# Window attention and two gated MLPs on one core: new planner constants, a new order, and rotated operand slots

## The chip, the cores and the metric

The program runs on one core of a Trainium2 chip. The metric is device time in microseconds (us) of one execution; lower is better. Engines are named as in the profile: PE (matrix products), DVE (vector), ACT (activations, with function tables that have to be loaded), POOL (a slower second vector engine), SP (issues the DMAs). Each engine works through its own queue in order and waits on semaphores for the others.

## What is computed

The reference is windowed causal attention (4 batches, 8 heads, 576 positions, head size 64, window 128, a linear bias by head), then two MLPs over the 2304 x 512 result, with 2048 hidden features each:

```python
scores = np.where(mask, scale * q @ k.T + bias, -1e9)      # mask: 0 <= i - j < 128
attn = exp(scores - max) / (sum + 1e-9);  x = attn @ v     # heads side by side: 2304 x 512
h = x @ w_in;  x = (h * np.tanh(softplus(h))) @ w_out       # first MLP
h = x @ w_in2; x = np.where(h > 0, h, np.exp(h) - 1) @ w_out2  # second MLP
```

## The kernel before

**Products.** All MLP products are done in a two-level scheme with 7 products of half-size blocks in place of 8 (steps P1 to P7, in the order P1, P5, P6, P2, P7, P3, P4). Each factor is split into a high and a low part in a rounded float32 type, and three partial products (high-high, high-low, low-high) are summed. So every operand of PE needs a first half, the rounded copy (ACT, or DVE), and a second half, the difference (DVE, or POOL where both are in SBUF). `split` (L540) emits the two; `copy` (L528) and `combine` (L533) give the engines that may do them.

**Stages.** Attention of batch 0 comes first (`unit`, L687: scores, two transposes, values). Then the hidden products of the first MLP run over 4 chunks of tokens, one per batch (blocks H00 to H03, `hidden`, PE line L914, six matmuls of 288 columns a block), with the attention of the next batch between them. Next come the outward products of the first MLP in 3 chunks (O00 to O02, `outward`, PE line L1001, twelve matmuls of 384 columns a block), the hidden products of the second MLP (H10 to H12, L914 with 384 columns), and its outward products (O10 to O12). The hidden results go through DRAM (`gate`, `graw`); in the first MLP ACT applies Mish to them when they come back (L978). A block's name ends in its step: O00P5 is step P5 of outward chunk 0.

**Weights.** `convert` (L583) turns the packed 64-bit input words into float32 weights: a load, a Prelu on ACT (L593), a Copy on ACT or DVE (L597), a shift on DVE (L601), an add on POOL or DVE (L604), then four sums of blocks (DVE or POOL). Groups c0 to c3 are the four weight matrices; c0 is done at the start, the others beside the chunks. `load_weights` (W1 to W3) brings the finished ones back and splits them.

**Order.** Nothing is written out by hand in its final order. `Plan` collects about 4,100 operations with the engines that may do each (`ways`), a cost, a due time, a size for DMAs, and the function table that an ACT operation needs. `Plan.order` then runs a list scheduler over a model of the engines, whose choices set the order of each queue and the engine of each operation with more than one way. The model's constants are `LATENCY`, `LOAD`, `RATE` and the `*_cost` functions; the preferences are the table `AT`; and `SHIFT` adds a number to the priority of each group of operations. Where PE would idle in the first 90 us of the model, it gets products of constants that nobody reads (L489).

**Slots.** Buffers come from rings of slots; the next buffer of a ring takes the next slot, and its first writer waits until the last reader of the slot's former buffer is done. The split operands of the outward products (`hl`) use ring "L", with 5 slots: three on the right (numbers 4 to 6 of `right_s`), then two on the left (4 and 5 of `wide_s`). The first step of chunk 0 uses ring "L0", the same three slots on the right alone:

```python
    plan.ring("L0", right_s[4:])
    plan.ring("L", right_s[4:] + wide_s[4:])
```

Of ACT's operations, Exp is entered with the table "exp" and Mish with "mish"; the Prelu of `convert` is entered with none.

## Time and profile before

| | |
|---|---|
| time, median of 3 runs | 868.26 us (867.78 to 868.77) |
| time of the profiled execution | 868.03 us |
| its span, first to last instruction | 866.3 us |
| PE busy | 843.4 us, 97% |
| DVE busy | 723.1 us, 83% |
| ACT busy | 628.3 us, 73% |
| POOL busy | 132.4 us, 15% |
| PE share of the chain that ended last | 70% |

The time of the profiled execution is 1.73 us above its span. Busy PE counts matmuls that overlap each other, so a block of 12 matmuls of 384 columns is best timed from the start of one block to the start of the next.

### The profile page before, as it was taken

Reading aid. Unit: us, or ns where it says so; the run is one execution under the profiler, and the core shown is the slowest. Engines: PE = TensorE matmul, PEld = TensorE weight load, DVE = VectorE, ACT = ScalarE, POOL = GpSimd, SP = SyncE. Lnnn points to the kernel's source line nnn. Section 1 sums busy time; section 2 is a strip of 40 time slices with the busy share of each in tenths; the row PEclk is TensorE's granted clock in tenths of the full one; section 3 lists DMA queues with packets and bytes.
Section 4 is the critical chain, followed back from the end, with each engine's and each line's share of the span. In section 5 each row is a group of like instructions: output and inputs, shape, how many; then the busy total and the mean of one; then the engine's idle time right before and its main releaser. Section 6 shows DMA issues by size and latency. Waiting matters only on the chain.

```text
span 866.3 us, 15682 instructions
## 1 busy us (share of the span) xinstructions
PE 843.4 (97%) x5403; PEld 794.1 (92%) x5403; DVE 723.1 (83%) x1590; ACT 628.3 (73%) x1421; POOL 132.4 (15%) x115
## 2 busy tenths in 40 slices
PE   9988999999999999899899999999999999999998
PEld 6767788898889999899899999989999999999998
DVE  8999998778877689799889988895978988877863
ACT  6989997677767688875897868976998944333442
POOL 0434120000003000135213043121300000000000
PEclk9999999999999999999999999999999999999999
DMA  7436667877867886674677778676778957226102
GB/s 277 138 119 214 190 211 244 280 267 258 253 225 246 286 290 235 233 254 149 232 264 258 254 249 284 218 266 214 261 253 275 313 182 229 105 96 229 41 1 73
DMA packets 85967, 187.67 MB, mean 217 GB/s; under 512 B 8576, under 2 KB 30080, under 8 KB 85888
## 3 DMA queue, kind: packets, MB, share of 16 engines
q1 hardware_dynamic: 85888, 186.68, 64.2%
q8 instruction: 42, 0.69, 0.3%
q14 instruction: 37, 0.30, 0.1%
HBM read 117.44 MB, written 69.21 MB: 215 GB/s over the span
## 4 chain that ended last, share of the span: by engine, by line
PE 70%; DVE 12%; ACT 11%; DMA 3%; issue 3%; POOL 0%; SPq 0%; DVEq 0%; ACTq 0%; POOLq 0%
PE oA L1001 19%; PE hA L914 16%; PE oC L1001 11%; PE hC L914 8%; PE hB L914 4%; PE oB L1001 4%; PE ps_o L828 3%; DMA raw<-in_w_dram 2%; PE ps_s L725 2%; DVE hl L534 2%; PE ps_t L780 2%; DVE graw L534 1%; ACT hl L529 1%; ACT p L745 1%; ACT p L760 1%
## 5 line engine op out<-in xcount | busy, mean ns | idle before, releaser
L914 PE MATMUL hA<-xt,w 128*128 128x288 f32 (+1 forms) x1344 | 232.9, 319 | 2.3 <-ACT g L529 1.7
L529 ACT ACTIVATE hl<-graw 128x768 fp32r<-128x768 f32 x161 | 134.9, 843 | 128.1 <-PE oA L1001 63.8
L1001 PE MATMUL oA<-hl,w 128*128 128x384 f32 x1152 | 215.2, 338 | 4.2 <-DVE hl L534 2.4
L914 PEld LDWEIGHTS hA<-xt,w 128*128 128x128 f32 x1344 | 209.4, 189 | 8.0 <-ACT g L529 3.7
L534 DVE TENSOR_TENSOR hl<-graw,hl 128x768 fp32r<-128x768 f32 x168 | 165.8, 996 | 52.7 <-ACT hl L529 52.3
L1001 PEld LDWEIGHTS oA<-hl,w 128*128 128x128 f32 x1152 | 202.6, 188 | 7.0 <-DVE hl L534 4.8
L914 PE MATMUL hC<-xt,w 128*128 128x288 f32 (+1 forms) x672 | 119.7, 317 | 0.2 <-DVE g L897 0.2
L1001 PE MATMUL oC<-hl,w 128*128 128x384 f32 x576 | 111.0, 343 | 4.3 <-DVE hl L534 2.4
L1001 PEld LDWEIGHTS oC<-hl,w 128*128 128x128 f32 x576 | 103.0, 190 | 6.7 <-DVE hl L534 4.1
L914 PEld LDWEIGHTS hC<-xt,w 128*128 128x128 f32 x672 | 104.6, 188 | 3.0 <-issue 1.0
L534 DVE TENSOR_TENSOR graw<-graw 128x768 f32<-128x768 f32 x96 | 92.7, 977 | 4.2 <-ACT graw L978 1.8
L604 POOL TENSOR_TENSOR bits<-bits,raw 128x512 int32<-128x512 int32 x34 | 56.1, 1655 | 254.0 <-DVE bits L601 134.7
L529 ACT ACTIVATE g<-hA 128x288 f32<-128x288 f32 (+1 forms) x144 | 61.0, 434 | 26.6 <-PE hA L914 25.3
L745 ACT ACTIVATE p<-p,st 128x128 f32<-128x128 f32 x144 | 56.4, 396 | 13.8 <-DVE st L741 13.3
L534 DVE TENSOR_TENSOR w<-w 128x512 fp32r<-128x512 f32 x84 | 59.3, 730 | 6.2 <-ACT w L529 5.6
L914 PE MATMUL hB<-xt,w 128*128 128x288 f32 (+1 forms) x336 | 60.5, 317 | 2.4 <-DVE g L897 2.1
L914 PEld LDWEIGHTS hB<-xt,w 128*128 128x128 f32 x336 | 52.5, 188 | 4.2 <-DVE g L897 2.4
L1001 PE MATMUL oB<-hl,w 128*128 128x384 f32 x288 | 54.3, 338 | 0.0
L1001 PEld LDWEIGHTS oB<-hl,w 128*128 128x128 f32 x288 | 50.9, 188 | 0.2 <-DVE hl L534 0.2
L529 ACT ACTIVATE w<-w 128x512 fp32r<-128x512 f32 x83 | 49.3, 625 | 1.2 <-DMA w<-w_in 1.0
L896 ACT ACTIVATE e<-e 128x384 f32<-128x384 f32 x96 | 49.1, 529 | 0.7
L593 ACT ACTIVATE raw<-raw 128x512 f32<-128x512 f32 x64 | 43.0, 675 | 8.0 <-DMA raw<-in_w_dram 7.5
(100 smaller groups left out, 1109.2 us busy)
## 6 DMA issues: line engine op xcount, KB each, us to landing
graw<-gate SPq DMA_DIRECT2D x96, 384.0 KB, 4.6
raw<-in_w_dram SPq DMA_DIRECT2D x64, 512.0 KB, 5.3
gate<-g SPq DMA_DIRECT2D x64, 288.0 KB, 3.6
gate<-g SPq DMA_DIRECT2D x48, 384.0 KB, 3.9
w<-w_out SPq DMA_DIRECT2D x56, 256.0 KB, 4.0
qkv<-in_qkv_dram SPq DMA_DIRECT2D x16, 512.0 KB, 4.9
w_out<-bits SPq DMA_DIRECT2D x32, 256.0 KB, 5.1
w<-w_in SPq DMA_DIRECT2D x28, 256.0 KB, 3.7
```

What stands on the lines that cost most here:

```text
L529: ways = [("act", act_cost(n, sbuf), lambda: nc.scalar.activation(o(), i(), AF.Copy), 0.0), ("dve", dve_cost(n, sbuf), lambda: nc.vector.t ...
L534: emit = lambda eng: eng.tensor_tensor(out=o(), in0=x(), in1=y(), op=op)
L593: act(DM, lambda raw=raw: nc.scalar.activation(raw()[:, :, 1].bitcast(F32), raw()[:, :, 1].bitcast(F32), AF.Prelu, scale=2.0 ** -112, alph ...
L604: add = lambda eng, raw=raw, bits=bits: eng.tensor_tensor(out=bits().bitcast(I32), in0=bits().bitcast(I32), in1=raw()[:, :, 0].bitcast(I32 ...
L725: nc.tensor.matmul(pss[j]()[:, n, w0:2 * P], qs()[rs, n * P:(n + 1) * P], ks()[rs, ko + w0:ko + 2 * P], start=n == 0, stop=True, skip_grou ...
L745: act(P, lambda n=n, j=j: nc.scalar.activation(prob()[:, n, j], prob()[:, n, j], AF.Exp, scale=-1.0, bias=st()[:, 0, n, j:j + 1], accum_ou ...
L760: ("act", act_cost(P, True, 1), lambda y=y, f=f: nc.scalar.activation(y(), y(), AF.Copy, scale=f()), AT["norma"]),
L780: nc.tensor.transpose(ps()[:, j], prob()[:, n, j], ident)
L828: nc.tensor.matmul(o()[j * D:(j + 1) * D, c0:c0 + math.prod(y.shape[1:])], vn()[:kr, n, j], y, start=n == 0, stop=n == nkb - 1, skip_group ...
L896: act(T, lambda: nc.scalar.activation(e(), e(), AF.Relu, scale=-1.0, bias=1.0), (), [e], due)
L914: nc.tensor.matmul(ps(), w()[:, a, wi, cs], x()[:, b, k], start=step in FIRST and k == 0 and m == 0, stop=k == 1 and m == 2, skip_group_ch ...
L1001: nc.tensor.matmul(bk[name, d](), w()[:, a, wi, cs], x()[:, b, k], start=step in FIRST and f + k == 0 and m == 0, stop=f + k == NQ - 1 and ...
```

## The change

The kernel's operations are the same; the engine of some of them, their order, and the slots of `hl` differ. The change replaces all of `SHIFT`, and some of `AT` (`turn` 0.99 to 7.6, the price of a table load; `held` 10.7 to 102.2, the price of starting a DVE operation that shares a port while POOL works; `ahead`, `kappa`, `lag`, `dma`). In the model all latencies grow by 0.05 us, a DMA issue costs 0.43 us in place of 0.1, data land 0.45 us later behind their issue, and the DMA rate rises from 270 to 390 KB a us. The Prelu of `convert` is now entered with the table "exp". Ring "L" becomes one ring for each outward layer, "La" and "Lb", which begin at different slots.

```diff
-AT = dict(... turn=0.99, held=10.7, ... kappa=1.29, lag=0.9, ... dma=-14.73, ... ahead=7.48, hb=5)
+AT = dict(... turn=7.60436, held=102.159, ... kappa=1.35238, lag=0.940919, ... dma=-7.29047, ... ahead=-153.07, hb=5, lrot=2)
 SHIFT = {
-    "H000P1": -7.2, "H001P1": 4.9, "H001P6": 13.2, "H002P4": -0.5, "H002P6": -1.8, "H003P7": 0.4, "H003d": 11.8,
+    "H000P1": -15.5, "H000P2": 52.4, "H000P3": -45.1, "H000P4": -13.3, "H000P5": -21, "H000P6": -39.5, "H000P7": -1.9,
...
-    LATENCY = dict(pe=0.2, act=0.16, dve=0.13, pool=0.1, sp=0.0)
+    LATENCY = dict(pe=0.25, act=0.21, dve=0.18, pool=0.15, sp=0.05)
-    WARM = 6.9
+    WARM = 4.0
-    LOAD = 1.4
-    RATE, OUTSTANDING, LANDING = 270e3, 8, 1.9
+    LOAD = 1.3
+    RATE, OUTSTANDING, LANDING = 390e3, 8, 1.9
-                        dma_free = max(dma_free, end + 0.3) + o["moved"] / self.RATE
+                        dma_free = max(dma_free, end + 0.75) + o["moved"] / self.RATE
...
-    plan.ring("L", right_s[4:] + wide_s[4:])
+    ls, lr = wide_s[4:] + right_s[5:] + right_s[4:5], int(AT["lrot"])
+    plan.ring("La", ls)
+    plan.ring("Lb", ls[lr:] + ls[:lr])
...
-        plan.op([("sp", 0.1, emit, 0.0)], reads, writes, due=due, moved=moved * slow)
+        plan.op([("sp", 0.43, emit, 0.0)], reads, writes, due=due, moved=moved * slow)
...
                 raw()[:, :, 1].bitcast(F32), raw()[:, :, 1].bitcast(F32), AF.Prelu, scale=2.0 ** -112, alpha=-2.0 ** 32),
-                (), [(raw, 1)], due)
+                (), [(raw, 1)], due, extra=0.5, table="exp")
...
-                x = buf("L0" if at_end else "L1" if layer and ci == 0 and i == 0 else "L", (2, 2, T), F32R, "hl")
+                x = buf("L0" if at_end else "L1" if layer and ci == 0 and i == 0 else ("La", "Lb")[layer], (2, 2, T), F32R, "hl")
```

Numbers of instructions: POOL's tensor operations go from 105 to 94, ACT's activations from 1266 to 1238, DVE's operations from 1446 to 1485 (two-part ones counted once), the unread products on PE from 155 to 146, and ACT's table loads behind the first from 10 to 14. Rounded copies of `hl` on DVE (CAST hl) go from 7 to 23.

**Place 1: PE at the start of the first outward stage.** oA, oB and oC are the accumulators of the steps: the first four blocks on oA are P1, those on oC P5, the next on oA P6. Before:

```order
L914 MATMUL hC<-xt,w 128x288 x6
L1001 MATMUL oA<-hl,w 128x384 x12
L914 MATMUL hA<-xt,w 128x288 x6
L1001 MATMUL oA<-hl,w 128x384 x36
L1001 MATMUL oC<-hl,w 128x384 x24
L1001 MATMUL oA<-hl,w 128x384 x12
L1001 MATMUL oC<-hl,w 128x384 x12
```

In the changed kernel the same stretch reads:

```order
L956 MATMUL hA<-xt,w 128x288 x6
L1043 MATMUL oA<-hl,w 128x384 x24
L1043 MATMUL oC<-hl,w 128x384 x12
L1043 MATMUL oA<-hl,w 128x384 x12
L1043 MATMUL oC<-hl,w 128x384 x12
L1043 MATMUL oA<-hl,w 128x384 x12
L1043 MATMUL oC<-hl,w 128x384 x24
```

P1 was four blocks in a row (with one hidden block among them) ahead of the first P5; now P5 blocks stand between the P1 blocks, on slots that the rotated ring gives them.

**Place 2: ACT's table loads between the rounded copies of `hl`.** The queue of ACT at the second and third load of the kernel before (graw is the Mish on hidden results, raw the conversion of weights):

```order
L529 ACTIVATE hl<-graw 128x768
L593 ACT_TABLE_LOAD
L593 ACTIVATE raw<-raw 128x512
L597 ACTIVATE raw<-raw 128x512
L529 ACTIVATE hl<-graw 128x768
L593 ACTIVATE raw<-raw 128x512
L597 ACTIVATE raw<-raw 128x512
L978 ACT_TABLE_LOAD
L978 ACTIVATE graw<-graw 128x768
L529 ACTIVATE hl<-graw 128x768
```

In the changed kernel the first pair of loads that stands among the outward blocks of this chunk:

```order
L571 ACTIVATE y<-oA 128x384 x2
L635 ACT_TABLE_LOAD
L635 ACTIVATE raw<-raw 128x512
L571 ACTIVATE hl<-graw 128x768 x2
L1020 ACT_TABLE_LOAD
L1020 ACTIVATE graw<-graw 128x768
L571 ACTIVATE hl<-graw 128x768
```

and, in the second chunk, the densest group of loads in it:

```order
L571 ACTIVATE hl<-graw 128x768 x2
L1020 ACT_TABLE_LOAD
L1020 ACTIVATE graw<-graw 128x768 x2
L639 ACTIVATE raw<-raw 128x512
L635 ACT_TABLE_LOAD
L635 ACTIVATE raw<-raw 128x512
L1020 ACT_TABLE_LOAD
L1020 ACTIVATE graw<-graw 128x768 x2
L571 ACTIVATE hl<-graw 128x768 x2
```

A load is now kept apart from its neighbours by copies of `hl` in the first chunk; in the second, three loads stand without a copy of `hl` between them.

**Place 3: POOL's first work behind its setup.** Before:

```order
L604 TENSOR_TENSOR bits<-bits,raw 128x512 x2
L534 TENSOR_TENSOR sums<-bits 128x256
L604 TENSOR_TENSOR bits<-bits,raw 128x512
L534 TENSOR_TENSOR bits<-bits 128x256
L534 TENSOR_TENSOR w<-bits,w 128x512 x2
L534 TENSOR_TENSOR sums<-bits,sums 128x256 x2
L534 TENSOR_TENSOR xc<-xc 128x2x288
```

In the changed kernel:

```order
L646 TENSOR_TENSOR bits<-bits,raw 128x512
L576 TENSOR_TENSOR w<-bits,w 128x512
L576 TENSOR_TENSOR w<-sums,w 128x512
L576 TENSOR_TENSOR w<-sums,w 128x256
L576 TENSOR_TENSOR w<-bits,w 128x512
L576 TENSOR_TENSOR sums<-bits 128x256
L646 TENSOR_TENSOR bits<-bits,raw 128x512
```

Adds and sums of the first conversions have gone from POOL's queue to DVE's. Counted up to what the last block of hidden chunk 0 (H007P4) needs, POOL has 24 operations in place of 30, DVE 410 instructions in place of 400, ACT 289 in place of 294, and on PE that block is the 155th in place of the 152nd (unread products left out).

## Rows read from the trace of the kernel before

**Rows 1.** Windows by stage: length, busy us (instructions) by engine, PE clock, DMA share, GB/s
```profile
0.00:130.00 130.00, 122.19 (x969) 97.01 (x970) 122.28 (x487) 114.36 (x380) 35.96 (x40) 1.00 0.57 192
130.00:310.00 180.00, 179.73 (x1406) 162.99 (x1405) 140.30 (x466) 130.96 (x386) 13.47 (x11) 1.00 0.78 258
310.00:500.00 190.00, 183.62 (x1024) 180.79 (x1023) 171.06 (x207) 151.66 (x219) 41.64 (x30) 0.99 0.71 240
500.00:681.00 181.00, 177.95 (x999) 176.33 (x999) 151.49 (x266) 151.95 (x329) 41.31 (x34) 0.99 0.76 254
681.00:866.00 185.00, 179.88 (x1012) 176.99 (x1010) 137.95 (x168) 79.33 (x112) 0.00 (x0) 1.00 0.39 134
```

**Rows 2.** PE's waits from 310 to 510 us: total us, times, longest
```profile
PE oC L1001 <- DVE hl L534: 2.1, 3, 1.3
PE oC L1001 <- ACT hl L529: 1.9, 2, 1.0
PE oA L1001 <- ACT hl L529: 1.8, 1, 1.8
PE oA L1001 <- DVE hl L534: 0.6, 1, 0.6
```

**Rows 3.** Timeline of PE, 300 to 345 us: start, us, operation, count, idle before
```profile
312.98 6.51 PE L1001 MATMUL oA<-hl,w 128*128 128x384 f32 x36
320.42 0.44 PE L1001 MATMUL oC<-hl,w 128*128 128x384 f32 x1 [0.93 <-ACT hl L529]
321.42 5.85 PE L1001 MATMUL oC<-hl,w 128*128 128x384 f32 x23 [0.56 <-DVE hl L534]
```

**Rows 4.** Windows beside and in the two clock dips (columns as in group 1)
```profile
322.00:325.50 3.50, 3.50 (x13) 3.50 (x12) 3.50 (x5) 3.31 (x5) 0.00 (x0) 0.51 1.03 394
325.50:331.00 5.50, 5.50 (x33) 5.50 (x33) 4.80 (x6) 3.66 (x6) 0.00 (x0) 1.00 1.05 406
584.90:588.30 3.40, 3.40 (x13) 3.40 (x12) 1.59 (x3) 1.61 (x5) 0.00 (x0) 0.50 0.95 298
```

**Rows 5.** Timeline of all engines, 345 to 361 us
```profile
345.47 1.28 ACT L593 ACT_TABLE_LOAD   x1
346.76 0.69 ACT L593 ACTIVATE raw<-raw 128x512 f32<-128x512 f32 x1
349.88 1.28 ACT L978 ACT_TABLE_LOAD   x1
355.75 0.44 PE L1001 MATMUL oC<-hl,w 128*128 128x384 f32 x1 [1.00 <-ACT hl L529]
357.44 2.21 PE L1001 MATMUL oC<-hl,w 128*128 128x384 f32 x11 [1.25 <-DVE hl L534]
```

**Rows 6.** Timeline of all engines, 414 to 430 us
```profile
417.83 1.28 ACT L593 ACT_TABLE_LOAD   x1
420.38 1.28 ACT L978 ACT_TABLE_LOAD   x1
424.77 0.44 PE L1001 MATMUL oA<-hl,w 128*128 128x384 f32 x1 [1.76 <-ACT hl L529]
425.76 2.18 PE L1001 MATMUL oA<-hl,w 128*128 128x384 f32 x11 [0.55 <-DVE hl L534]
```

**Rows 7.** Timeline of all engines, 574 to 586 us
```profile
580.80 1.47 POOL L604 TENSOR_TENSOR bits<-bits,raw 128x512 int32<-128x512 int32 x1
581.05 2.04 DVE L534 TENSOR_TENSOR x<-x 128x768 f32<-128x768 f32 x1
583.61 1.32 PE L914 MATMUL hB<-xt,w 128*128 128x384 f32 x6 [2.09 <-DVE g L897]
```

**Rows 8.** PE's waits from 681 us to the end
```profile
PE oA L1001 <- DVE hl L534: 1.9, 3, 1.0
PE oC L1001 <- DVE hl L534: 0.2, 1, 0.2
```

**Rows 9.** Groups by line and form: busy us, mean ns of one, idle before
```profile
L529 ACT ACTIVATE hl<-graw 128x768 fp32r<-128x768 f32 x161 | 134.9, 843 | 128.1 <-PE oA L1001 63.8 <-PE oC L1001 39.5 <-PE oB L1001 11.5
L534 DVE TENSOR_TENSOR hl<-graw,hl 128x768 fp32r<-128x768 f32 x168 | 165.8, 996 | 52.7 <-ACT hl L529 52.3
L593 ACT ACT_TABLE_LOAD x5 | 6.4, 1283 | 0.4 <-DMA raw<-in_w_dram 0.3
L534 DVE TENSOR_TENSOR sums<-bits,sums 128x256 f32<-128x256 f32 x17 | 7.6, 446 | 0.1
L534 DVE TENSOR_TENSOR w<-sums,w 128x512 fp32r<-128x512 f32 x6 | 4.1, 678 | 0.0
```

More of the change, by code (lines that the diff above doesn't have):

```diff
@@ L20 @@
 GROUPS = ((0, 256, 0, 256), (256, 256, 128, 384), (512, 64, 384, 192))
-AT = dict(copy=2.27, both0=-0.71, both1=-8.32, both2=-3.61, turn=0.99, held=10.7, fill=90, enough=1.5, norma=-0.5, normp=2.42,
-          kappa=1.29, lag=0.9, first=-64.52, unit=2.69, h1=50.67, chunk=70.1, lead=30.24, dt=1.35, dma=-14.73,
-          conv=-27.63, wadd=-0.1, soft0=0, soft1=0, soft2=0, soft3=0, eq=4, ep=2, et=6, er=3, eb=0, eraw=3, side0=1,
-          side1=2, depth=4, ahead=7.48, hb=5)
+AT = dict(copy=2.27, both0=-0.71, both1=-8.32, both2=-3.61, turn=7.60436, held=102.159, fill=90, enough=1.5, norma=-0.5,
+          normp=2.42, kappa=1.35238, lag=0.940919, first=-64.52, unit=2.69, h1=50.67, chunk=70.1, lead=30.24, dt=1.35,
+          dma=-7.29047, conv=-27.63, wadd=-0.1, soft0=0, soft1=0, soft2=0, soft3=0, eq=4, ep=2, et=6, er=3, eb=0,
+          eraw=3, side0=1, side1=2, depth=4, ahead=-153.07, hb=5, lrot=2)
 SHIFT = {
[55 rows of a table removed]
[95 rows of a table added]
 class Slot:
@@ L362, in mm_cost @@
 def mm_cost(n):
-    return 0.000417 * n + (0.0125 if n < 384 else 0.0153)
+    return 0.000417 * n + (0.013 if n < 384 else 0.0158)
 def act_cost(n, sbuf=False, extra=0):
-    return 0.000833 * n + 0.052 + 0.041 * sbuf + 0.093 * extra
+    return 0.000833 * n + 0.049 + 0.041 * sbuf + 0.093 * extra
 def dve_cost(n, fast=False, extra=0):
-    return (0.00052 if fast else 0.001042) * n + 0.068 + 0.062 * extra
+    return (0.00052 if fast else 0.001042) * n + 0.068 + 0.067 * extra
 def pool_cost(n):
@@ L591, in convert @@
             dma(P * DM * 8, lambda raw=raw, s=s: nc.sync.dma_start(out=raw().rearrange("p n w -> p (n w)"), in_=s),
[L592 removed]
+                (), [(raw, 0), (raw, 1)], due, 1.15)
             act(DM, lambda raw=raw: nc.scalar.activation(
                 raw()[:, :, 1].bitcast(F32), raw()[:, :, 1].bitcast(F32), AF.Prelu, scale=2.0 ** -112, alpha=-2.0 ** 32),
[L595 removed]
+                (), [(raw, 1)], due, extra=0.5, table="exp")
             ends_of = lambda raw=raw: (raw()[:, :, 0].bitcast(I32), raw()[:, :, 0])
[L597 removed]
+            plan.op([("act", act_cost(DM, True, 0.5), lambda ends_of=ends_of: nc.scalar.activation(*ends_of(), AF.Copy, scale=2.0 ** -29), 0.0),
                      ("dve", dve_cost(DM, True), lambda ends_of=ends_of: nc.vector.tensor_scalar(
@@ L606, in convert @@
             plan.op([("pool", pool_cost(DM), lambda add=add: add(nc.gpsimd), 0.0),
-                     ("dve", 0.16 + 0.00104 * DM, lambda add=add: add(nc.vector), AT["wadd"])],
+                     ("dve", 0.07 + 0.00104 * DM, lambda add=add: add(nc.vector), AT["wadd"])],
                     [(raw, 0)], [bits, (bits, 0), (bits, 1)], due=due, port=True)
@@ L640, in convert @@
                 out=to, in_=(t() if n == 3 else t().bitcast(F32).rearrange("p (n c) -> p n c", n=2))),
-                [have[x][1] for x in which.split()], [("wsd", w, q, x) for x in which.split()], due, 1.2)
+                [have[x][1] for x in which.split()], [("wsd", w, q, x) for x in which.split()], due)
     def weight_slots(w):
@@ L699, in unit @@
         t = buf("qkv" + late, (cut[3],), F32, "qkv")
-        dma(P * cut[3] * 4, lambda: nc.sync.dma_start(out=t(), in_=src), (), [t], t0 - 10)
+        dma(P * cut[3] * 4, lambda: nc.sync.dma_start(out=t(), in_=src), (), [t], t0 - 10, 1.08 if part == 1 else 1.0)
         qs, ks, vs = ((lambda i=i: t()[:, cut[i]:cut[i + 1]]) for i in range(3))
```

2 lines of the change are left out of this document (removed), and 148 rows, old and new, of the table SHIFT.

## The prediction

> **What bounds the kernel now.** I read the windows by stage first [rows 1]. PE is busy almost throughout: from 130 to 310 us it misses 0.27 us of 180. So a new order of the same work can only win what PE loses elsewhere: 130 - 122.19 = 7.8 us before 130 us, 190 - 183.62 = 6.4 us in the first outward stage (310 to 500), 181 - 177.95 = 3.05 us in the second hidden stage, and in the last stage the 2.1 us of waits that are listed [rows 8]; the rest of that stage's idle time is the ending, which the change does not touch. To this come two dips of the granted clock to half, at 322 to 325.5 and at 584.9 to 588.3 us [rows 4]. Full speed beside the first is 33 matmuls in 5.5 us, 0.167 us each; 3.5 us would give 21, and 13 stand there, so a dip costs 8 x 0.167 = 1.3 us. Each followed idle PE: 0.93 us ahead of 320.42 and 0.56 ahead of 321.42 [rows 3], and 2.09 ahead of 583.61 [rows 7].
>
> In the first 130 us the queues behind PE are full themselves: DVE is busy 122.28 us, ACT 114.36 [rows 1]. There DVE and ACT, not PE, set the pace.
>
> In the first outward stage PE's waits are all for the split operand hl [rows 2]: 2.1 + 1.9 + 1.8 + 0.6 = 6.4 us, the whole loss. They are three places.
> (a) At 320 us: 0.93 + 0.56 = 1.5 us and the dip of 1.3 [rows 3, 4]. Ring L0 has three slots, so the fourth P1 operand takes the first slot again; ring L begins with that slot too, so the first P5 operand cannot be made before PE has finished the block directly ahead. The path from one block to the next is then a rounded copy on ACT (0.84 us) and a difference on DVE (1.0 us) [rows 9], with nothing to hide them.
> (b) At 355 us: 1.00 + 1.25 us [rows 5]. Two table loads with two conversions of weights stand in ACT's queue just ahead; the old planner gave Prelu no table and did not know of them.
> (c) At 424 us: 1.76 + 0.55 us [rows 6], the same with the loads at 417.83 and 420.38.
> Together (b) and (c) are 4.6 us.
>
> **The change, part by part.** *Slots and order at the start of the stage (a).* The rotated ring gives the first P5 operands the two left slots, which no P1 operand used, and PE's queue now has P1, P1, P5, P1, P5. The fourth P1 operand still waits for the first P1 block, but two blocks lie between them. A block is 12 matmuls at 0.176 us (36 of them took 6.5 us with the drain at their end [rows 3]), about 2.1 us; two give 4.2 us of cover against 0.84 + 1.0 us of split plus handovers. So 1.5 us go, and the dip's 1.3 with them: -2.8 us. What is late next is DVE: differences, weight splits and sums of hidden blocks queue there, and summed along its queue it stays about 0.5 to 3 us ahead of PE through this chunk. Should that lead fail, the wait comes back at P7 of chunk 0.
>
> *Table loads (b, c).* The loads rise from 10 to 14, 4 x 1.283 = 5.1 us more work for ACT [rows 9]. ACT is busy 151.66 of 190 us here [rows 1], so the work itself fits. What counts is whether a load stands on the path to the next hl. In chunk 0 two copies of hl now stand between a load and the next. In chunk 1 the densest group has no hl for three loads, four Mish and two conversions. Mish takes about as long as the copy of hl (both 768 wide: 0.84 us, 0.75 taking the overlap of neighbours off), a conversion 0.69 [rows 5], about 0.56 the same way: 3 x 1.29 + 4 x 0.75 + 2 x 0.56 = 8 us. By the slots of the new order, the copy ahead of the group can start when a certain PE block ends, and the copy behind it only when the fourth block after that one ends: 4 x 2.1 = 8.4 us. So the group fits, narrowly. I take (b) and (c) as gone but for 1.5 us of new tight places: in chunk 2 two pairs of blocks (P7, P3) get their operand's slot only two blocks ahead, with splits of the next weights between them on DVE. With the 0.3 us of small waits kept, the stage keeps about 2.0 of its 7.7 us: -5.7 us. Bounds: all 7.7 gone, or the loads' extra 5.1 us on the path.
>
> *Second hidden stage.* The 2.09 us wait [rows 7] came from a DVE operation of 2.04 us beside a POOL operation, ahead of the gate that frees a PSUM bank. The order of that stage is another throughout, and DVE has about 4 us less in its queue there, done earlier, where DVE idled (140.30 busy of 180 us [rows 1]). Nothing ties the old wait to the new order, and nothing forbids a like one. Of 3.05 + 1.3 = 4.35 us I keep 2.0: -2.35. Bounds: -4.35 and 0.
>
> *Start of the last stage.* Of the 2.1 us [rows 8] I keep 1.0: -1.1. DVE has its first two hl operands ready earlier, but its queue runs within about 1 us of PE afterwards. Bounds: -2.1 and +1.
>
> *First 130 us.* POOL loses 6 operations up to the last block of hidden chunk 0, and DVE has 10 instructions more. Six at 0.45 to 0.68 us [rows 9], and four short ones at 0.2 to 0.3, make some 4.5 us. PE has three blocks more in front of that block (two or three of them hidden ones, about 3 us), so DVE's surplus over PE grows by about 1.5 to 2 us. Against it, POOL operations slow DVE: one took 2.04 us beside POOL [rows 7] and about 1.0 us is usual for its size [rows 9], so six fewer can give up to 6 us back. Fewer unread products (146 for 155) cost and bring nothing, since they fill idle PE. I take +1.0; bounds -4 and +3.7 (DVE's surplus and no relief).
>
> *The rest.* The cost and latency constants, the DMA issue time and rate are only in the model; they act through the order that is counted above. DMA loads keep their distance: counted in PE blocks between the one that frees a buffer and the one that needs it, the tightest weight load of the first outward stage has 6.4 us in both orders.
>
> Sum: -5.7 - 2.35 - 1.1 + 1.0 = -8.15 us. Against the profiled execution's 868.03 us (span 866.3) that is 859.9. The median of the runs is 0.2 us higher, less than these terms are known to.
>
> Where POOL's traffic slows DVE, the Trainium skill (GPSIMD Engine Reference, Key points) says that the two share their SBUF interfaces and that DVE instructions in a 2-port mode or with two SBUF inputs contend; the 2.04 us operation [rows 7] has two SBUF inputs and agrees.
>
> **The rivals.** *DVE becomes the bound (slower).* DVE gets 39 operations more. The places where it is nearly full are the first 130 us (94% busy) and the first outward stage (171.06 of 190, 90%) [rows 1], where 7 rounded copies of hl stand on it in place of 2. If POOL's relief fails, the early +3.7 comes out in full; and if the hl waits are DVE's (2.7 of the 6.4 us already are [rows 2]), then five more copies at about 0.6 us, 3 us, add to them and the waits stay. That is 868.0 + 3.7 + 3 = 874.7, or 870.9 with half of the stage's 7.7 us gone. It decides where DVE's idle time in the outward stage falls under about 10 us. For it: the shares named. Against it: the sum of DVE's queue between the stage's first blocks and its last is within 1 us of the old, as other work was moved ahead.
>
> *Loads on the path.* The order sets 14 loads for 10; with 5.1 us of them on the path to hl the result is 859.9 + 5.1 = 865.0. For it: the group of three in chunk 1. Against it: 8 us against 8.4. The Trainium skill (ScalarE: Activation LUTs, Table sets: the hidden batching unit) tells to do all work of one set together, which this order does less than the old. The same page (What ACT_TABLE_LOAD costs) puts a switch at 1283 ns and a drain of about 1380, which would make four switches 10.6 us, an estimate from that page, and the time 870.5; here the next ACTIVATE starts 1.29 us behind the load [rows 5], with no drain to be seen.
>
> *One stall for another.* PE's waits move to other blocks and sum to the same: 868, within 1.7.
>
> *More than I take.* All waits for hl and the gate go (7.7 + 4.35 + 2.1) and the early stretch gains 1: 868.03 - 15.1 = 852.9.
>
> **How the numbers follow.** Faster or slower by 0.2% (1.7 us) is about what a measurement of this kernel can tell from no change. The forecast as summed, 856 to 863: 0.50. Loads on the path: 0.10. More than I take: 0.15. One stall for another: 0.09. DVE the bound: 0.16. So faster 0.75, same 0.09, slower 0.16. The range goes from 851.5 (below the best case) to 870.0, and leaves out about half of the DVE case and little else.
>
> **What would show it.** In the profile of the changed kernel: no idle PE and no half clock at the first blocks on oC (if there is, the slot step was wrong); PE's waits for hl in the first outward stage at about 2 us, none behind a table load (if a wait for ACT's hl stands behind the group of three in chunk 1, the cover was counted wrong); PE's idle time in the second hidden stage near 2 us; DVE's idle time in the first outward stage well above 10 us; the last block of hidden chunk 0 within about 2 us of the old, three blocks of work allowed for. The prediction is wrong if DVE is late at most blocks of either full stretch, or if the first 130 us move by more than 4 us.

## The result and the profile after

The changed kernel takes 861.28 us (median of 8 runs, 859.09 to 865.26) against 868.38 us for the kernel before on the same chip (8 runs, 867.23 to 870.48): a ratio of 0.9917, interval 0.9895 to 0.9939. The profiled execution of after took 861.93 us (span 860.2), that of before 868.03 (span 866.3). So the pair of profiles that is read below differs by 6.1 us, the medians by 7.1.

Windows by stage of after, the answer to [rows 1]: length, busy us (instructions) of PE, PEld, DVE, ACT and POOL, PE clock, DMA share, GB/s. The last two rows stand where the two dips of [rows 4] stood.

```profile
0.00:130.00 130.00, 121.55 (x977) 98.38 (x978) 121.99 (x495) 114.10 (x377) 29.02 (x34) 1.00 0.56 190
130.00:310.00 180.00, 178.34 (x1397) 162.03 (x1396) 148.19 (x490) 137.38 (x394) 18.60 (x17) 1.00 0.88 293
310.00:500.00 190.00, 185.17 (x1040) 182.34 (x1039) 177.24 (x219) 152.06 (x216) 41.49 (x28) 1.00 0.70 234
500.00:681.00 181.00, 179.51 (x1018) 177.61 (x1017) 146.59 (x259) 147.32 (x322) 27.04 (x25) 1.00 0.70 240
681.00:860.00 179.00, 172.12 (x970) 169.85 (x968) 137.45 (x171) 67.05 (x93) 0.00 (x0) 1.00 0.36 126
320.00:332.00 12.00, 12.00 (x70) 12.00 (x70) 11.90 (x16) 11.99 (x22) 0.00 (x0) 1.00 1.05 405
582.00:592.00 10.00, 10.00 (x59) 10.00 (x58) 5.34 (x11) 6.94 (x16) 3.10 (x4) 1.00 0.48 172
```

Subtract PE's busy time from each length: PE is idle for 8.45, 1.66, 4.83, 1.49 and 6.88 us, where before it was 7.81, 0.27, 6.38, 3.05 and 5.12. The sum is 23.3 us against 22.6: **the idle time of PE did not fall**. What fell is its busy time, from 843.4 to 836.7 us on the two pages. Both dips are gone (the clock column is 1.00 in the last two rows). A dip is 3.5 us in which PE works at 1.2 GHz in place of 2.4, so it does 1.75 us of work too little: 3.5 us for the two. The unread products fell from 155 to 146, and their busy time from 23.2 to 21.2 us: 2.0. About 1.2 us is left; what it is was not settled (the ends of matmuls in a profile are modelled). This is the account of one pair of profiles, and single runs of the changed kernel differ from one another, as the second profile of it shows below.

The start of the first outward stage (PE's timeline: start, us, operation, count, idle before) answers [rows 3]: P1, P1, P5, P1, P5 without a gap.

```profile
309.76 4.41 PE L1043 MATMUL oA<-hl,w 128*128 128x384 f32 x24
314.01 2.27 PE L1043 MATMUL oC<-hl,w 128*128 128x384 f32 x12
316.12 2.28 PE L1043 MATMUL oA<-hl,w 128*128 128x384 f32 x12
318.24 2.27 PE L1043 MATMUL oC<-hl,w 128*128 128x384 f32 x12
```

PE's waits in that stage, 310 to 510 us (total us, times, longest), the answer to [rows 2]: the three places of before are gone, and nine waits stand there, the longest 1.1 us for 1.8. They sum to 6.0 us for 6.4; the wait for g, 1.1 us, comes behind 500 us.

```profile
PE oA L1043 <- DVE hl L576: 1.9, 4, 0.9
PE hA L956 <- ACT g L571: 1.1, 1, 1.1
PE oB L1043 <- DVE hl L576: 1.1, 1, 1.1
PE oC L1043 <- DVE hl L576: 0.7, 1, 0.7
PE oC L1043 <- ACT hl L571: 0.7, 1, 0.7
PE oA L1043 <- ACT y L571: 0.5, 1, 0.5
```

Where they come from is seen in the densest group of table loads. The timeline of all engines of after, 395 to 422 us, cut to what bears on hl:

```profile
400.89 0.85 ACT L571 ACTIVATE hl<-graw 128x768 fp32r<-128x768 f32 x1 [1.78 <-PE oA L1043]
400.96 0.43 SPq L633 DMA_DIRECT2D raw<-in_w_dram  x1
...
404.64 0.85 ACT L1020 ACTIVATE graw<-graw 128x768 f32<-128x768 f32 x1 [0.74 <-DMA graw<-gate]
...
406.19 2.07 DVE L576 TENSOR_TENSOR hl<-graw,hl 128x768 fp32r<-128x768 f32 x1
...
407.87 0.69 ACT L639 ACTIVATE raw<-raw 128x512 int32<-128x512 uint32 x1 [2.38 <-DMA raw<-in_w_dram]
...
413.35 1.56 ACT L571 ACTIVATE hl<-graw 128x768 fp32r<-128x768 f32 x2
...
414.23 0.44 PE L1043 MATMUL oC<-hl,w 128*128 128x384 f32 x1 [0.66 <-ACT hl L571]
...
415.36 4.29 PE L1043 MATMUL oC<-hl,w 128*128 128x384 f32 x23 [0.69 <-DVE hl L576]
```

From the copy at 400.89 to the one at 413.35 pass 12.5 us. They hold 9.3 us of work, the first copy's 0.85 included (the forecast counted 8, without that copy), and 3.1 us of waits (0.74 + 2.38) **for DMAs**: ACT works in order, so a conversion of a weight whose bytes have not landed holds every copy of hl behind it. The slot for the second copy was free at 409.3, four blocks on; the copy came 4 us later, and PE's lead absorbed all but the 0.66 + 0.69 us. (The split at 406.19 took twice its usual 1.0 us; a POOL operation of 1.50 us began at 405.94.) ACT's waits from 310 to 505 us show how common this is (total, times, longest). Two rows of after:

```profile
ACT raw L639 <- DMA raw<-in_w_dram: 7.9, 5, 3.2
ACT graw L1020 <- DMA graw<-gate: 3.5, 5, 1.0
```

and one of before (its Prelu has line 593):

```profile
ACT raw L593 <- DMA raw<-in_w_dram: 1.8, 1, 1.8
```

11.4 us in place of 2.1 (with 0.3 us of before ahead of a table load). What these waits cost PE does not follow from their sum, since ACT may have time to spare where it waits; the experiments below take them apart from the loads. The same kind of wait stands in the last stage on DVE: after's timeline, 704 to 728 us.

```profile
719.43 0.96 DVE L576 TENSOR_TENSOR graw<-graw 128x768 f32<-128x768 f32 x1 [1.97 <-DMA graw<-gate]
...
723.73 0.41 PE L1043 MATMUL oA<-hl,w 128*128 128x384 f32 x1 [1.52 <-DVE y L576]
...
724.97 2.20 PE L1043 MATMUL oA<-hl,w 128*128 128x384 f32 x11 [0.82 <-DVE hl L576]
```

The difference graw<-graw at 719.43 is for an operand of the next chunk; the split hl that PE wants at 724 stands behind it in DVE's queue. Before lost 2.1 us to waits of this stage [rows 8], after 3.3 (1.5 + 1.5 + 0.3 in its list of waits).

In the groups of after that answer the first two of [rows 9], one copy of hl takes 842 ns and one split 1005, within 1% of those of before, so nothing of the gain comes from faster copies and splits.

### The profile page after: what moved, and what is told of

The parts are those of the page before. It is cut to its first block, busy times and chain, and to the rows that moved or that the text cites. A ratio compares the mean times of both kernels' runs of the same rounds, so it can differ in the third digit from the quotient of the medians.

```text
span 860.2 us, 15671 instructions
## 1 busy us (share of the span) xinstructions
PE 836.7 (97%) x5394; PEld 790.2 (92%) x5394; DVE 731.5 (85%) x1629; ACT 617.9 (72%) x1397; POOL 116.2 (14%) x104
## 4 chain that ended last, share of the span: by engine, by line
PE 60%; DMA 13%; DVE 12%; ACT 7%; issue 6%; POOL 1%; SPq 1%; ACTq 0%; DVEq 0%; POOLq 0%
PE hA L956 20%; PE hC L956 10%; PE oA L1043 9%; PE oC L1043 5%; PE hB L956 5%; DMA graw<-gate 4%; DVE hl L576 3%; PE ps_o L870 3%; DMA qkv<-in_qkv_dram 3%; PE ps_s L767 2%; DVE graw L576 2%; DMA raw<-in_w_dram 2%; DVE w L576 2%; PE oB L1043 2%; PE ps_t L822 2%
## 5 line engine op out<-in xcount | busy, mean ns | idle before, releaser
L956 PEld LDWEIGHTS hA<-xt,w 128*128 128x128 f32 x1344 | 207.3, 188 | 9.7 <-ACT g L571 3.6
L571 ACT ACTIVATE hl<-graw 128x768 fp32r<-128x768 f32 x145 | 121.1, 842 | 111.1 <-PE oA L1043 58.0
L576 DVE TENSOR_TENSOR hl<-graw,hl 128x768 fp32r<-128x768 f32 x168 | 166.6, 1005 | 28.4 <-ACT hl L571 27.7
L1043 PE MATMUL oC<-hl,w 128*128 128x384 f32 x576 | 108.8, 339 | 1.7 <-DVE hl L576 1.0
L646 POOL TENSOR_TENSOR bits<-bits,raw 128x512 int32<-128x512 int32 x30 | 47.7, 1591 | 296.0 <-DVE bits L643 176.0
L787 ACT ACTIVATE p<-p,st 128x128 f32<-128x128 f32 x144 | 56.2, 395 | 10.6 <-DVE st L783 10.4
L576 DVE TENSOR_TENSOR w<-w 128x512 fp32r<-128x512 f32 x84 | 56.7, 698 | 1.6 <-ACT w L571 1.5
L802 ACT ACTIVATE p<-p,st 128x128 f32<-128x128 f32 x124 | 41.1, 396 | 8.9 <-DVE st L797 8.8
```

The costliest lines, as they stand in the source:

```text
L571: ways = [("act", act_cost(n, sbuf), lambda: nc.scalar.activation(o(), i(), AF.Copy), 0.0), ("dve", dve_cost(n, sbuf), lambda: nc.vector.t ...
L576: emit = lambda eng: eng.tensor_tensor(out=o(), in0=x(), in1=y(), op=op)
L646: add = lambda eng, raw=raw, bits=bits: eng.tensor_tensor(out=bits().bitcast(I32), in0=bits().bitcast(I32), in1=raw()[:, :, 0].bitcast(I32 ...
L787: act(P, lambda n=n, j=j: nc.scalar.activation(prob()[:, n, j], prob()[:, n, j], AF.Exp, scale=-1.0, bias=st()[:, 0, n, j:j + 1], accum_ou ...
L802: ("act", act_cost(P, True, 1), lambda y=y, f=f: nc.scalar.activation(y(), y(), AF.Copy, scale=f()), AT["norma"]),
L956: nc.tensor.matmul(ps(), w()[:, a, wi, cs], x()[:, b, k], start=step in FIRST and k == 0 and m == 0, stop=k == 1 and m == 2, skip_group_ch ...
```

## The experiments

For most of them the order of one kernel was written out as a list and played back instruction for instruction, so that nothing but the named edit differs. Labels that begin with b start from the kernel before, those with a from the changed one. A ratio is against the kernel before, measured beside it on the same chip. In small order diffs the names are those of the timeline.

**The changed kernel again, no edit.**

> The changed kernel once more, for a second trace of it and as the measure for its three variants. 861.3 us; if the wait on landing graw at 717 to 725 us is the order's, it stands again with 2 to 3 us of PE's time; if it is an accident of one run, it is under 1 us here.

862.03 us (7 runs, 860.79 to 871.18), ratio 0.9934 (0.9913 to 0.9954). The run that was profiled was the slowest, 871.18. Its three dips (windows, columns as above) and the idle time of PE ahead of them (PE's timeline):

```profile
176.00:179.50 3.50, 3.50 (x21) 2.80 (x18) 2.07 (x13) 0.60 (x3) 0.00 (x0) 0.52 0.96 321
514.00:517.50 3.50, 3.50 (x13) 3.50 (x12) 1.13 (x4) 1.01 (x2) 0.90 (x2) 0.53 0.91 302
732.50:736.00 3.50, 3.50 (x12) 3.50 (x13) 1.35 (x2) 0.00 (x0) 0.00 (x0) 0.53 1.02 336
```
```profile
174.41 1.05 PE L956 MATMUL hC<-xt,w 128*128 128x288 f32 x6 [1.46 <-DVE g L576]
512.95 4.98 PE L956 MATMUL hA<-xt,w 128*128 128x384 f32 x18 [2.53 <-ACT g L571]
731.24 0.42 PE L1043 MATMUL oA<-hl,w 128*128 128x384 f32 x1 [1.06 <-DVE y L576]
```

Most waits of the program stand again where they stood (the third row is the one of 723.73 above). The one of 512.95 was 1.13 us in the first profile, and the one of 174.41 was not there. The dips are all new: the same program had none in its first profile and three in this one. So dips belong to a run, and each of these came right after PE had been idle. The stretch that was full in before shows a difference too:

```profile
130.00:310.00 180.00, 175.81 (x1360) 158.66 (x1361) 145.64 (x485) 134.97 (x390) 18.45 (x17) 0.99 0.85 284
```

PE is idle there for 4.19 us in place of 1.66. In all eight profiles with the new order it is idle in this stretch for 1.66 to 4.99 us, in all six that start from before for 0.16 to 0.29. PE's waits name the landing of qkv in each of the eight (1.0 to 2.9 us, none in the six), and the wait for DVE's g that stands at 174.41 here is in five of them (1.1 to 1.7 us).

**(a), the slot alone.** The first P5 operands of the first outward layer get slots that no P1 operand used; the order stays.

```diff
-    plan.ring("L", right_s[4:] + wide_s[4:])
+    plan.ring("La", [the slots written out: w5 r5 r6 w4 r4, repeated; then as before])
```

> The kernel before with its order kept, instruction for instruction; only the slots of the split operand change: up to the 24th operand of the first outward stage the first left slot and the last right slot are exchanged, so that the first P5 operand takes a slot that no P1 operand used. Theory A, the slot alone makes place (a): the 1.5 us of idle PE at 320 to 322 us and the dip of the clock behind it go, -2.8 us, 866.0. Theory B, the queues of ACT and DVE, written in an order that counted on the old slot, hold the copy back: the idle time stays above 1 us and the total within 1 us of 869.

866.62 us (12 runs), ratio 0.9981 (0.9962 to 1.0). PE at the place of [rows 3], and the window there:

```profile
319.17 0.44 PE L1001 MATMUL oC<-hl,w 128*128 128x384 f32 x1 [0.46 <-ACT hl L529]
```
```profile
319.00:325.50 6.50, 5.78 (x31) 5.53 (x32) 5.81 (x8) 5.67 (x10) 0.00 (x0) 1.00 1.01 375
```

The slot alone takes a third of the 1.5 us of idle time (0.46 + 0.55 are left), and in this profile the first dip; the copy is still made right behind the block ahead. The changed kernel, which has the order P1, P1, P5 as well, has neither. The second dip stands (its granted clock is 0.57 from 582.5 to 586.5 us), and PE's idle time in the whole stage, 6.57 us, is that of before. About 2 us in the median, on the edge of what can be told from nothing.

**The dips alone.** Unread products are put into the two idle places of before (8 at 319 us, 18 at 581); the waits for data stay.

```diff
+  8 products of ones, unread, ahead of the first P5 block     (PE, line 489)
+ 18 products of ones, unread, ahead of the block at 583.61    (PE, line 489)
```

> The kernel before with 8 unread products more in PE's queue ahead of the first P5 block and 18 more ahead of the block that waits at 583.6 us; all else as it was. Theory A, the clock falls because PE is idle there: both dips go, -1.3 us each, 866.5, while the blocks' waits stay. Theory B, the dips have another cause: they stay, and the total is 869 or more by what the products delay.

867.92 us (12 runs), ratio 0.9992 (0.9974 to 1.0011). In the profile both places run at full clock:

```profile
322.00:325.50 3.50, 3.50 (x22) 3.50 (x21) 3.50 (x5) 3.01 (x5) 0.00 (x0) 1.00 1.02 390
582.00:592.00 10.00, 10.00 (x62) 9.88 (x61) 4.72 (x10) 6.12 (x14) 0.00 (x0) 1.00 0.71 245
```

So in this run PE, kept busy, keeps its clock there: 22 matmuls in 3.5 us against 13 [rows 4]. The total did not follow: in seven of the other eleven runs the mean clock was 0.995 to 0.998, so dips came in them too, at places that no trace shows. That the filling is what kept the clock is not shown by one profile, since the same idle places pass without a dip in other runs (next experiment). What a single dip's removal brings to the median stays open.

**The loads out of before.** Prelu becomes Copy, a function of the set that Mish uses: 8 of the 10 loads go, the order stays.

```diff
-  AF.Prelu, scale=2.0 ** -112, alpha=-2.0 ** 32)
+  AF.Copy, scale=2.0 ** -112)
```

> The kernel before in its order, with Copy in place of Prelu for the converted weights' upper halves, so that 8 of its 10 table loads behind the first fall away (left out: the sign of negative weights). Theory A, as I forecast: the stalls at 355 and 424 us were the loads', 2.3 us each; both shrink under 0.5 us, -4 to -4.6, 864.5. Theory B, they are DVE's or the order's: at most 1 to 2 us go, 867 to 868.

860.16 us (6 runs), ratio 0.9919 (0.9892 to 0.9947): as much as the whole change brings. First outward window, and the longest wait left, which is not followed by a dip:

```profile
310.00:500.00 190.00, 187.98 (x1063) 186.20 (x1062) 176.46 (x217) 144.69 (x217) 47.62 (x34) 1.00 0.73 248
```
```profile
576.04 1.33 PE L914 MATMUL hB<-xt,w 128*128 128x384 f32 x6 [2.07 <-DVE g L897]
```
```profile
577.00:580.50 3.50, 3.50 (x22) 3.41 (x21) 1.92 (x4) 2.33 (x5) 0.00 (x0) 1.00 0.99 302
```

Idle PE in the stage falls from 6.38 to 2.02 us, of which 1.5 us are place (a), as in before:

```profile
319.49 0.44 PE L1001 MATMUL oC<-hl,w 128*128 128x384 f32 x1 [0.93 <-ACT hl L529]
```

That (b) and (c) come from the loads is shown: of the 4.6 us counted 0.5 is left. The median falls by 8.6 us. Part of that is dips: between runs at full clock on this chip it is 5.7 us (865.5, four runs, and 859.9, four runs). The profile of this run has no dip: PE goes on at full clock after 2.07 us of idle time, where 2.09 us in before was followed by one [rows 7, 4], and also after the 0.93 + 0.56 us of place (a), which a dip followed in before and in the run without POOL's traffic, and none here or in the run with only the count.

**The loads out of after.** The same edit in the changed kernel: 2 loads for 14.

> The changed kernel's order, instruction for instruction, but the converted weights' upper halves go through Copy in place of Prelu, so that ACT keeps Mish's table and 12 of the 14 loads behind the first fall away (left out: the sign of negative weights). Theory A, loads on the path to hl: the stalls at 364, 414 and 420 us in the first outward stage shrink, together 2 to 4 us, total 857.5 to 859.5. Theory B, loads hidden as I forecast but for 1.5 us of other tight places: within 1 us, 860.5 to 861.5.

860.86 us (6 runs), ratio 0.9907 (0.9887 to 0.9927).

```profile
310.00:500.00 190.00, 188.16 (x1067) 186.04 (x1066) 178.86 (x224) 138.02 (x206) 42.45 (x28) 1.00 0.71 240
```

Idle PE in the stage is 1.84 us in place of 4.83: the loads, with what they delay, still cost the changed kernel 3 us there. ACT's waits for landing DMAs did not fall with it. They are 14.6 us in place of 11.4 (7.8 in this row, 5.6 for graw and 1.2 ahead of the Prelu), 3.4 of them in the same group of ACT's queue (here from 404.97 us on), behind which PE no longer waits:

```profile
ACT raw L639 <- DMA raw<-in_w_dram: 7.8, 5, 3.2
```

So behind this group the landings alone are hidden; PE waited there for landings and loads together. The total hardly shows the 3 us; in the profiled run, the slowest of the six, the stretch from 130 to 310 us was idle for 4.86 us in place of 1.66.

**Only the count.** One word in the planner of before: the Prelu has a table. The planner makes a new order, with 12 loads.

```diff
-                (), [(raw, 1)], due)
+                (), [(raw, 1)], due, table="exp")
```

> The kernel before with one edit: the planner is told that Prelu needs the table of Exp, so that it counts the loads; its constants, rings and table of numbers stay, and the planner writes a new order (12 loads behind the first in place of 10). Theory A, counting alone spaces the loads as I forecast for (b) and (c): -3 to -5 us, 864 to 866. Theory B, the counting does little without numbers fitted to it, since each load moved makes another wait: within 2 us of 869, or slower.

863.95 us (5 runs), ratio 0.9949 (0.9928 to 0.9971).

```profile
310.00:500.00 190.00, 185.35 (x1039) 181.56 (x1038) 171.75 (x213) 151.85 (x218) 47.53 (x34) 1.00 0.72 241
```

Idle PE in the stage is 4.65 us, near the changed kernel's 4.83, without the new times, shifts and slots; place (a) stands in it with its 0.93 + 0.56 us, as in before. The one word gives 4.75 of the 7.1 us in the medians, two thirds (by the interval of its ratio, 2.5 to 6.3 us). Only some 2 us of it stand between runs at full clock (865.7, two runs, and 863.7, three); the rest is fewer dips.

**POOL out of before.** POOL's in-place additions work on 16 columns in place of all.

```diff
-  lambda: emit(nc.gpsimd)
+  lambda: nc.gpsimd.tensor_tensor(out=o()[..., :16], in0=x()[..., :16], in1=y()[..., :16], op=op)
```

> The kernel before in its order, with POOL's in-place additions (53 of its 105) on 16 columns in place of 256 to 576 (left out: the rest of these sums). Theory A, the 2.09 us wait at 583.6 us is made by POOL's addition beside DVE's subtraction: it falls to about 1 us, and with it the dip goes, -2.3 us in the second hidden stage; the first 130 us win 1 to 3 us as I took for POOL's relief; total 864 to 866. Theory B, POOL's relief is nothing in the first 130 us, as in the same edit of the changed kernel: only the second hidden stage wins, 866 to 867.5.

861.38 us (6 runs), ratio 0.9925 (0.99 to 0.9951).

```profile
0.00:130.00 130.00, 124.22 (x985) 98.93 (x985) 119.07 (x494) 115.40 (x385) 25.05 (x41) 1.00 0.59 195
500.00:681.00 181.00, 180.24 (x1022) 178.83 (x1021) 149.07 (x273) 157.37 (x338) 19.29 (x34) 1.00 0.80 262
```
```profile
576.16 0.94 DVE L534 TENSOR_TENSOR x<-x 128x768 f32<-128x768 f32 x1
```

The operation of 2.04 us beside POOL [rows 7] takes 0.94 us, its wait is gone, and PE's idle time falls by 2.3 us in the second hidden stage (3.05 to 0.76) and by 2.0 in the first 130 us (7.81 to 5.78), where DVE's busy time falls from 122.28 to 119.07. In the first 130 us part of this is the run: with only the slots changed, at a later place, PE was idle there for 6.61 us. That POOL's traffic slows DVE is shown. The 7.4 us of the median are not its price alone, since POOL's own operations end earlier too, and what waits for them. The Trainium skill (GPSIMD Engine Reference, Key points) says that the two share SBUF interfaces and that a DVE instruction with two SBUF inputs contends; the pair 2.04 and 0.94 us agrees.

**POOL out of after.** The same edit.

> The changed kernel's order, but POOL's in-place additions (46 of its some 95) work on 16 columns in place of 256 to 576 (left out: the rest of these sums). Theory A, POOL slows DVE and DVE's split operands come late for it: the 0.9 us stall at 420 us goes, where one subtraction took 2 us beside POOL, and the first 310 us win 1 to 3 us; total 858 to 860. Theory B, POOL's traffic is not on the path: within 1 us, 860.5 to 861.5.

858.93 us (4 runs), ratio 0.9888 (0.9868 to 0.9908): 2 to 3 us less than after. In the first 130 us PE is busy 123.45 us in place of 121.55; DVE's busy time in the first outward stage falls from 177.24 to 168.60, and PE's idle time there from 4.83 to 3.44. So POOL's share in the waits of the changed kernel is real and smaller than in before.

**The old last stage in the new kernel.** The operations of the last stage stand in the order and slots of before. SP's queue just ahead of the stage, part of the difference:

```diff
 L988 DMA gate<-g 128x768
 L721 DMA w<-w_out 128x512 x2
-L988 DMA gate<-g 128x768
-L721 DMA w<-w_out 128x512
+L1016 DMA graw<-gate 128x768
+L988 DMA gate<-g 128x768
+L721 DMA w<-w_out 128x512
```

(A - row is not in this kernel, a + row is added; the rows alternate in this way over some 30 DMAs.)

> The changed kernel up to the last stage; the last stage's operations in the order, on the engines and in the slots of the kernel before. Theory A, the last stage's new order loses 3 us at 717 to 725 us since the loads of graw for its second chunk start at 707 us, and the old order starts them some 10 us earlier: DVE's wait for graw goes, total 858.5 to 859.5. Theory B, the loss is DVE's queue, late in any order: 861.0 to 862.5.

875.39 us (6 runs), ratio 1.0082 (1.006 to 1.0104). A miss by its seam: loads of graw came to stand ahead of loads of weights in SP's queue, and the weights came late.

```profile
672.25 2.29 PE L956 MATMUL hA<-xt,w 128*128 128x384 f32 x6 [7.91 <-DVE g L576]
```
```profile
ACT w L571 <- DMA w<-w_out: 7.2, 1, 7.2
```

It does not answer what the stage's order costs. It does show the mechanism at its largest: one load that ACT's next operation needs is late by 7.2 us, and PE is idle for 7.91.

**Waiting operations moved behind splits.** In the changed kernel 14 operations of ACT and DVE that wait for a DMA are put behind copies and splits of hl that were ready (at 361, 395, 408 and 717 us). ACT's queue there, a part:

```diff
 L1020 ACTIVATE graw<-graw 128x768 x2
-L571 ACTIVATE hl<-graw 128x768
+L571 ACTIVATE hl<-graw 128x768 x2
 L639 ACTIVATE raw<-raw 128x512
```

> The changed kernel with 14 operations of ACT and DVE moved a few places back in their queues, at 361, 395 and 408 us (converted raw and Mish behind the copies of hl) and at 717 us (the differences of the next chunk behind the splits of this one); nothing else changes but that one pair of table loads falls away with it. Theory A, PE waits there because an operation that waits for its transfer stands ahead of a split in a queue that works in order: the stalls at 364, 396 to 403, 411 to 424 and 720 to 725 us, 7.5 us in the trace of the changed kernel, shrink to under 3, total 857 to 858.5. Theory B, DVE's amount of work makes them, and they return a block later: within 1 us of the changed kernel, 860.5 to 862.

861.18 us (6 runs), ratio 0.9916 (0.9895 to 0.9937): nothing in the total. The last stage did what was expected, its waits fell from 3.3 to 1.9 us. In the first outward stage they came back at other blocks, the longest of them:

```profile
420.30 3.72 PE L1043 MATMUL oA<-hl,w 128*128 128x384 f32 x11 [0.91 <-DVE hl L576]
```

These 11 matmuls took 3.72 us in place of 2.2: a dip. ACT's waits for landing raw and graw in the stage fell from 11.4 to 6.8 us (the row below and 0.5 for graw), PE's idle time only from 4.83 to 4.27; ahead of the block shown, three Mish had come to stand before two copies of hl.

```profile
ACT raw L639 <- DMA raw<-in_w_dram: 6.3, 4, 3.0
```

**Five more moved.** The same, with three weight splits and two copies of y on DVE moved behind splits of hl.

```diff
-L576 TENSOR_TENSOR hl<-graw,hl 128x768
+L576 TENSOR_TENSOR hl<-graw,hl 128x768 x2
 L576 TENSOR_TENSOR w<-w 128x512
 L572 COPY y<-oC 128x384
-L576 TENSOR_TENSOR hl<-graw,hl 128x768
```

> The kernel a_dma with five more operations moved: at 451 and 467 us and at 704 us the split that PE waits for goes ahead of splits of later weights and of a copy on DVE. Theory A, the 1.05, 0.42 and 0.47 us stalls there are the order's: 1 to 2 us less than a_dma. Theory B, DVE is behind by its work: same as a_dma within 0.5 us.

861.57 us (6 runs), ratio 0.9921 (0.9898 to 0.9944). No different from the run before it; PE's waits in the stage fell from 4.2 to 3.3 us, less than the runs scatter.

**What worked, together.** The changed kernel with 11 operations moved, at 408, 451, 704 and 717 us only, and one pair of table loads joined with another (12 for 14). ACT and DVE, a part of each:

```diff
 L639 ACTIVATE raw<-raw 128x512
+L571 ACTIVATE hl<-graw 128x768
 L635 ACT_TABLE_LOAD
 L635 ACTIVATE raw<-raw 128x512
+L571 ACTIVATE hl<-graw 128x768
+L639 ACTIVATE raw<-raw 128x512
+L635 ACTIVATE raw<-raw 128x512
```
```diff
-L576 TENSOR_TENSOR hl<-graw,hl 128x768
-L576 TENSOR_TENSOR graw<-graw 128x2x384
-L576 TENSOR_TENSOR hl<-graw,hl 128x768
+L576 TENSOR_TENSOR hl<-graw,hl 128x768 x2
+L576 TENSOR_TENSOR graw<-graw 128x2x384
```

> The changed kernel with 11 operations moved: at 408 us (one Prelu behind a copy of hl; the other Prelu, which joins its pair of table loads; three Mish and one difference behind the copies and splits of this chunk), at 451 us (one split ahead of a weight's split and a copy), at 704 and 717 us (splits ahead of weights' splits and ahead of the next chunk's differences, which wait for graw). Left as in the changed kernel, against a_dma: 361 and 395 us, where the waits came back a few blocks later, and no Mish ahead of the two copies at 418 us. Theory A, the waits at 411 to 424 us (3 us), at 452 us (1.3) and at 717 to 725 us (2.9 in the trace of the changed kernel) are the order's and go: 4 to 6 us by these stalls, total 857 to 859. Theory B, only the last stage's goes, as in a_dma, and the first outward stage refills its waits: 859.5 to 861.5.

859.61 us (6 runs, 857.08 to 861.17), ratio 0.9881 (0.9857 to 0.9906).

```profile
310.00:500.00 190.00, 186.91 (x1057) 184.59 (x1056) 177.29 (x222) 149.85 (x216) 43.76 (x28) 1.00 0.71 238
681.00:857.90 176.90, 172.47 (x976) 171.15 (x975) 137.86 (x172) 66.66 (x93) 0.00 (x0) 1.00 0.37 127
```
```profile
415.68 4.39 PE L1043 MATMUL oC<-hl,w 128*128 128x384 f32 x24
```
```profile
DVE graw L576 <- DMA graw<-gate: 1.1, 2, 0.9
```

The block at 415.68, ahead of which the changed kernel waited twice (0.66 and 0.69 us), waits for nothing; PE's idle time in that stage falls from 4.83 to 3.09 us. In the last stage DVE's wait of 1.97 us is gone, and the idle time falls from 6.88 to 4.43. Only swaps at two places of DVE's queue do that, at 704 and at 717 us. Those at 717 take the splits out from behind the difference that waits, and the 1.52 + 0.82 us of PE behind it become 0.46 (0.82 in the run with 14 moved, which has these too). So that order is shown as the cause there; in the outward stage the moves and the joined loads act together. The kernel computes the whole result and is the fastest of them; against the kernel before that is settled, against the changed one likely (about 2 us; the two intervals overlap by 0.0011).

## Why the prediction was right and wrong

The total was right: forecast 859.9 us, measured 861.28, and the likeliest case's 856 to 863 holds it. The terms were less right, and made it up between them, which was luck. The stages below are those of the one pair of profiles.

**Up to the first outward stage: +1.0 forecast, about -1.1 in the pair.** The second P1 block begins at 309.76 + 2.1 = 311.9 us, before at 312.98 [rows 3]. The first block of attention on PE starts at 4.52 us in place of 5.93, which I did not look for: the change also reorders SP's first loads. The DVE surplus did not come out: the last block of hidden chunk 0 ended 0.7 us later (130.9 for 130.2), with three more blocks ahead of it. Against that, the stretch from 130 to 310 us, full before, now idles 1.66 us for 0.27. The step that failed is "a new order of the same work can only win what PE loses elsewhere": it left out that a new order can lose where nothing was lost, and this stretch got no term. The pair shows 1.4 us of it, the other profiles of the new order up to 4.7, with the landing of qkv in each. And the -1.1 is luck of this profile: in the six whose order is the same up to there, the second P1 block begins at 311.4 to 316.9 us (two of them with a dip on the way), 314.3 in the mean, against 312.2 to 313.0 in three with the order of before. By these the forecast of +1.0 was not too high.

**First outward stage: -5.7 forecast, about -3.3 measured** (idle 6.38 to 4.83, and one dip of 1.75). The slot step (a) was right: no idle PE, no half clock at the first blocks on oC, and DVE's lead held. The old stalls (b) and (c) are gone too. The step that failed is the cover of the load group, "3 x 1.29 + 4 x 0.75 + 2 x 0.56 = 8 us" against "4 x 2.1 = 8.4 us". It left out the copy ahead of the group, which starts where the cover starts: with it the work was 9.3 us, over the cover by itself. And it took what stands in ACT's queue as work only: ACT's waits for landing DMAs, 3.1 us in that group and 11.4 in the stage, were not in the sum. The loads and the waits act together: with the loads gone the stage idles 1.84 us under longer waits (14.6), with the waits at 6.8 us and the loads kept it idles 4.27. How the 2.8 us over the forecast divide between the two stays open. I looked at DMA loads only for the buffers that PE blocks free and need, not for what stands behind the waiting conversion. The new tight places were sized at 1.5 us and the stage's rest at 2.0; the stage kept 4.8. The place at 453 us that I had named, weight splits ahead of a split of hl on DVE, is there (1.1 us, the oB row of the waits).

**Second hidden stage: -2.35 forecast, about -3.3 measured** (idle 3.05 to 1.49, and a dip). Its mechanism, a DVE operation beside POOL, was shown by the run without POOL's traffic. The size is off by the dip.

**Last stage: -1.1 forecast, about +1.8 measured** (idle 5.12 to 6.88). The bound was +1. The failed step is "DVE has its first two hl operands ready earlier, but its queue runs within about 1 us of PE afterwards": it took the queue as work, but a difference for the next chunk waits for its DMA ahead of this chunk's splits, 1.97 us. It is the same blind spot as in the two stages before, and the last kernel shows that it goes with a swap.

**The dips.** Two at 1.3 us were counted, from missing matmuls in a window; 3.5 us at half the clock is 1.75 each, and the runs grouped by clock (below) give about 1.5. And that "each followed idle PE" was read as if a dip went with that idle place, which the runs contradict: see below.

**The sum.** -1.1 - 3.3 - 3.3 + 1.8 = -5.9, for -6.1 between the profiles and -8.15 in the forecast. Over-forecast in the first outward stage and the last (2.4 + 2.9 us) was offset by the early start (2.1) and the second hidden stage (1.0). The low end was summed inconsistently: the terms' own bounds (7.7, 4.35, 2.1 and 4 us) reach 849.9, below the 851.5 given; nothing came near it.

**The rivals.** *Loads on the path* was partly true: without the loads the stage of the changed kernel idles 1.84 us for 4.83, so 3 of its 5.1 us stand there, together with the waits in the group. *One stall for another* describes the idle time well (22.6 and 23.3 us) and the total not, since the busy time fell. *DVE the bound* did not come: DVE's idle time in the first outward stage is 190 - 177.24 = 12.8 us, above the 10 named. A part of its early loss may be there: the six profiles above begin the second P1 block 1.6 us later in the mean than the three, and in five of the eight PE waits for DVE's g at about 174 us. *More than I take* did not come either.

## What to carry to other kernels

When a reordering puts an instruction that waits for a DMA ahead of one that feeds the critical engine, count the landing and not only the work: in an in-order queue everything behind it waits too. Here that made PE wait 2.3 us in the last stage, and in the first outward stage, with the table loads, part of the 4.8 us where 2.0 were forecast. Tell a planner of every cost that its engine has before tuning the rest; one missing word was about two thirds of this change in the median. Where one engine's work doubles another's durations, look for the critical engine's short waits behind them. And take a second profile of the same program before a stage's loss or gain is put down to the order: one stretch here idled for 1.66 us in one and 4.19 in the other.

## What the runs showed of the hardware

**Half-clock stretches are drawn by the run.** The changed kernel shows none in one profile and three in the other of these stretches of about 3.5 us at 1.2 GHz in place of 2.4; one of them lowers the mean clock of a run by 0.002. Grouped by that, 53 of the 57 runs of the kernel before in the experiments take 866.0 us at 1.00 (9 runs), 868.0 at 0.998 (16), 869.1 at 0.996 (12) and 870.4 at 0.994 (16): about 1.5 us for each dip. The profiles hold eleven dips ahead of the end. Ten came right behind idle PE (the longest gap 0.87 to 2.53 us), one began within 7.91 us of it, yet 2.07 us of idle time also passed without one. The changed kernel ran at 1.00 in 10 of 15 runs, with a mean of 861.1 us. So of the 7.1 us, 4.9 stand between runs without any dip (not all on the same chips), and the rest is fewer dips. The pair of profiles, less two dips of 1.75 us, differs by only 2.6 us, so it does not show where all of the 4.9 come from. Why the changed kernel has fewer dips, with as much idle time in sum, was not settled either; its gaps are not always the shorter ones (1.13 us the longest from 310 to 681 us in its first profile, 2.53 in its second, 2.09 in before).

**A 512 KB load of weights took 5.5 us from issue to landing**, the median over 64 in the profile of after. The one issued at 400.96 us let ACT go on at 407.87, 6.9 us later. The Trainium skill (DMA: Bandwidth & Descriptors, Anatomy of one DMA) fits 2.0 us and the bytes at 436 GB/s for DMAs that GpSimd issues, which is 3.2 us for this size, an estimate from that page. The loads here are issued by SP, with the DMA engines 70 to 88% busy from 130 to 681 us, and took longer than that.
